# A kernel with its column product by seven products, and its operations placed by engine time

## The chip, the cores and the metric

The kernel runs on one core of a Trainium2 chip. The metric is the device time of one execution in microseconds: 985.84 us, the median of three runs (985.45 to 986.24). The page and the trace are those of one profiled execution.

## The reference, cut to what matters

```python
S, D, F = 2048, 640, 1536            # float32 throughout
xn = layernorm(x)                    # x: [S, D]
a  = xn @ dft_hid_re.T               # the product over the columns (real, imaginary)
b  = xn @ dft_hid_im.T
s  = dft_seq_re @ a - dft_seq_im @ b # the product over the rows
g  = silu((silu(xn @ w_gate) * (xn @ w_up)) @ w_down)
out = x + s * g
```

The kernel exchanges the two transforms: it multiplies by the rows' matrices first and by the columns' after.

## The kernel before, in words

**Number format.** TensorE multiplies float32r operands. Each operand is split into a high part (ACT, `split`, L196: a copy into float32r) and a low part (DVE, L201 or L203: the operand minus its high part). A product of two split operands is three matmuls (`mm3`, L217 to L219): high by high, high by low, low by high.

**Stages, in the order in which PE works.** All products are on transposed tiles of 128 partitions by `TC` = 512 columns; `j` is 0 or 1 and takes chunks `j` and `j + 2` of the 2048 rows.

- `seq(0)` to `seq(3)`: the product over the rows, by the seven-product (Strassen) scheme, for the two halves `j` and for the real and imaginary matrix. Left operands come from `in_cs`; some are added to a tile by accumulating loads that POOL issues (L581). The results go to `p_dram`.
- `hid(j)`: the product over the columns. For each of two chunks it takes ten blocks of `p_dram` (five real, five imaginary) by the five column blocks of the DFT matrix (`in_hd`), ten by five products, and adds them up in five PSUM banks. The right sides are loaded and split again for each `j`. The results go to `y_dram`.
- `gate_up(j)`: the two products with `w_gate` and `w_up` by the seven-product scheme, in twelve rounds `f`. Its left side, the layer-normed input, is made by `xn_t(j)`; `gate_weights` adds and splits each round's weights. In the rounds of `j` = 0 the generator `spare` also makes the operands of `w_down` and stores them (`d_p...` and `d_d...`).
- `down(j)`: the product with `w_down` by the function `strassen` (products p1, p2, p5, p6, p3, p7, p4; next to p1, p2, p5 and p4 runs a "direct" product for the fifth column block, with d1, d2, d1 and d3), whose weights SP fetches back (`fetch`, L1017). Each result passes a silu on ACT, is multiplied by the tile from `y_dram` and added to x on DVE, and is stored.

The order is hid(0), gate_up(0), down(0), hid(1), gate_up(1), down(1).

**What sets the order.** Nothing runs when it is recorded. `Plan` collects every operation with a time: `step` is a piece of PE's work at the running clock `now` (0.226 us for each matmul), `prod` an operation `lead` microseconds ahead of `now`, `post` one behind it. The leads are written by hand (`split(9, ...)`, `LEAD`, `OPEN_T`). `add` moves an operation back only as far as its data demands. The operations, sorted by these times, are issued in that order to the in-order queues of the engines; SP and POOL issue the transfers. Nothing waits for its planned time: an instruction runs as soon as its queue reaches it and its data and buffer are there. `place` and `fit` give each buffer an address in an arena ("hl" for split operands, "raw" for the rest) by the planned lifetimes; a buffer that takes the bytes of an older one waits until that one's last reader is done. Normalised x (`xn`, 40 KB of each partition) lies in "raw".

**The end of hid and the start of gate_up.** gate_up's first two products go to banks 7 and 6, and its third to bank 7 again, so the first product must have been evicted by ACT (L245) by then.

Of the kernel before, what the change touches and what calls it, by code (L numbers as in the profile page):

```python
# [22 lines left out]
MM = 0.226  # L23
HL_KB, RAW_KB, TURN_KB = 83, 95, 28


class Plan:

    def __init__(self):
        self.ops, self.size, self.wrote, self.read = [], {}, {}, {}
        self.now = 0.0
# [8 lines left out]
    def add(self, when, fn, reads=(), writes=(), hold=0.0):  # L45

        reads, writes = list(reads), list(writes)
        t = when
        for k in reads:
            t = max(t, self.wrote.get(k, t))  # L50
        for k in writes:
            t = max(t, self.wrote.get(k, t), self.read.get(k, t))
        for k in reads:
            self.read[k] = max(t, self.read.get(k, t))
        for k in writes:
            self.wrote[k] = t
        names = {k[:2] if k[1] in ("h", "l") else k[0] for k in reads + writes}
        self.ops.append((t, len(self.ops), fn, names, t + hold))
        return t

    def prod(self, lead, fn, reads=(), writes=(), hold=0.0):
        self.add(self.now - lead, fn, reads, writes, hold)

    def step(self, n, fn, reads=(), writes=()):
        t = self.add(self.now, fn, reads, writes, n * MM)
        assert t <= self.now + 1e-6, (t, self.now, [k for k in reads if self.wrote.get(k, 0) > self.now])
        self.now += n * MM

    def post(self, fn, reads=(), writes=(), after=0.0, hold=0.0):
        self.add(self.now + after, fn, reads, writes, hold)  # L70

    def place(self, limits):
# [8 lines left out]
        where = {}  # L81
        for arena, limit in limits.items():
            mine = [(n, self.size[n][1], *v) for n, v in life.items() if self.size[n][0] == arena]
# [9 lines left out]
            found = [f for f in (self.fit(sorted(mine, key=o), limit, p) for p, o in tries) if f]  # L93
# [3 lines left out]
            order, last = best[3], best  # L97
            for _ in range(24):
                hurt = sorted((n for n in last[2] if last[2][n] > 9), key=lambda n: -last[2][n])
                moved = {n: i for i, n in enumerate(hurt[:6])}  # L100
                order = sorted(order, key=lambda m: moved.get(m[0], 99))
                last = next((f for f in (self.fit(order, limit, pauses[a:]) for a in range(len(pauses))) if f), None)
                if last is None:
                    break
                best = min(best, last, key=lambda f: f[0])
            where |= best[1]
        return where

    @staticmethod
    def fit(mine, limit, pauses):  # L110

        placed, where, cost = [], {}, {}
        for n, size, ta, ia, tb, ib in mine:
            near = sorted((o, e, xa, ja, xb, jb) for o, e, xa, ja, xb, jb in placed
                          if (ja <= ib and ia <= jb) or (xa < tb + 8 and ta < xb + 8))
            for pause in pauses:
# [22 lines left out]
def tile_fnet_swiglu(  # L139
# [16 lines left out]
    nc = tc.nc  # L156
# [18 lines left out]
    def raw(name, a=0, n=None):  # L175
        o = where[name]
        arena, size = pl.size[name]
        return space[arena][:, o + a:o + (size if n is None else a + n)]

    def hl(name, i, a=0, n=None):  # L180

        key = name, "hl"[i]
        o = where[key]
        arena, size = pl.size[key]
        return space[arena][:, o + a:o + (size if n is None else a + n)]

# [68 lines left out]
    def strassen(tag, groups, get, top, dop, result, end=False):  # L255
# [16 lines left out]
        def operand(p, g, src):  # L272
# [3 lines left out]
            split(9, s, n, lambda: raw(name, a, n), [key])  # L276
# [13 lines left out]
        def accumulate(dst, src, n):  # L290
            (dn, da, dk), (sn, sa, sk) = dst, src
            pl.prod(12, lambda: nc.vector.tensor_tensor(raw(dn, da, n), raw(dn, da, n), raw(sn, sa, n), op=ALU.add),
# [40 lines left out]
        def s_1(g):  # L333
            X[g], V[g] = get(21, g), get(22, g)
# [7 lines left out]
        def s_2(g):  # L342
            accumulate(W[g], Y[g], n[g])
            return operand("p6", g, W[g])
# [5 lines left out]
        def s_3(g):  # L350
            accumulate(Y[g], X[g], n[g])
# [19 lines left out]
        def a22(g):  # L371
# [769 lines left out]
```

## Time and profile before

| | |
|---|---|
| median of three runs | 985.84 us |
| the profiled execution's own time | 985.85 us |
| its span (first to last instruction) | 984.1 us |
| mean granted TensorE clock | 1.000 |
| matmul instructions (PE) | 4300 |
| DMA | 184.54 MB, mean 188 GB/s |
| transfers that SP issues (queue q1) | 131.35 MB |
| transfers that POOL issues (queue q0) | 52.45 MB |

How to read the answers that are quoted below: a group's row has the line of the kernel, engine, operation, what it writes and reads, its shape, how often it runs, its busy time in us and the mean ns of one, then the idle time of that engine just before these instructions and what ended it. A row of the stretches has start and end in us, then the busy time of PE, PEld, DVE, ACT and POOL (with counts), the granted clock, the DMA share and GB/s. A row of the timeline has start, duration, engine, line, operation, shapes and, in brackets, the idle time before it and its releaser. "SPq" is the queue in which SP issues transfers; "to landing" runs from issue to the last byte.

### The profile page before, as it was taken

The page shows a single profiled execution, that of the slowest core. Times are in us where ns is not written, and L with a number is a line of the kernel's source. Part 1 is how long each engine was busy: PE and PEld are TensorE (multiplying, and loading weights), DVE is VectorE, ACT ScalarE, POOL GpSimd, SP SyncE. Part 2 cuts the span into 40 slices and gives each one's busy share as a digit, 9 for nine tenths or more (in the row PEclk, how much of TensorE's full clock was granted, in tenths as well). Part 3 has the DMA queues.
Part 4 walks back from the last instruction along what each step waited for, and adds up shares of the span by engine and source line. Part 5 has one row for each costly group of instructions (what it writes and reads, how often), then busy time and mean ns, then how long its engine had stood idle before and what let it go on. Part 6 is the DMA issues. An engine that isn't in the chain of part 4 may idle for free.

```text
span 984.1 us, 11734 instructions
## 1 busy us (share of the span) xinstructions
PE 976.2 (99%) x4300; PEld 803.5 (82%) x4300; DVE 700.2 (71%) x936; ACT 483.8 (49%) x706; POOL 106.5 (11%) x173
## 2 busy tenths in 40 slices
PE   9999999999999999999999999999999999999998
PEld 5888888888888888888788888888888888888886
DVE  6889769656865686377678887596578566665675
ACT  5786446444555464334655555343335544444342
POOL 0460220011001100010111211000010000000000
PEclk9999999999999999999999999999999999999999
DMA  9986788474848487540636547679950311125674
GB/s 340 289 209 178 232 243 253 147 210 121 228 141 222 121 238 241 205 172 25 219 134 231 203 144 250 215 242 353 302 204 27 107 55 54 53 75 176 194 264 185
DMA packets 73977, 184.54 MB, mean 188 GB/s; under 512 B 6720, under 2 KB 23360, under 8 KB 73920
## 3 DMA queue, kind: packets, MB, share of 16 engines
q1 hardware_dynamic: 59808, 131.35, 40.1%
q0 software_dynamic: 14112, 52.45, 18.6%
q8 instruction: 33, 0.54, 0.2%
q14 instruction: 24, 0.20, 0.1%
HBM read 149.42 MB, written 34.36 MB: 187 GB/s over the span
## 4 chain that ended last, share of the span: by engine, by line
PE 99%; DVE 0%; ACT 0%; issue 0%; DVEq 0%
PE ps L217 33%; PE ps L219 33%; PE ps L218 33%; PE ps L460 1%; PE ps L228 1%; DVE hl L201 0%; ACT L1088 0%; ACT raw L245 0%; DVE hl L203 0%; DVE raw L1059 0%; DVE raw L1061 0%; ACT hl L196 0%; ACT raw L1055 0%; DVE raw L914 0%; ACT z L1088 0%
## 5 line engine op out<-in xcount | busy, mean ns | idle before, releaser
L196 ACT ACTIVATE hl<-raw 128x1024 fp32r<-128x1024 f32 (+7 forms) x499 | 361.1, 766 | 299.4 <-PE ps L219 79.1
L201 DVE TENSOR_TENSOR hl<-raw,hl 128x1024 fp32r<-128x1024 f32 (+5 forms) x428 | 377.0, 908 | 142.6 <-ACT hl L196 75.8
L217 PE MATMUL ps<-hl 128*128 128x512 f32 x1088 | 422.4, 388 | 0.0
L219 PE MATMUL ps<-hl 128*128 128x512 f32 x1088 | 422.0, 388 | 0.0
L218 PE MATMUL ps<-hl 128*128 128x512 f32 x1088 | 422.0, 388 | 0.0
L218 PEld LDWEIGHTS ps<-hl 128*128 128x128 f32 x1088 | 204.3, 188 | 42.3 <-issue 0.2
L217 PEld LDWEIGHTS ps<-hl 128*128 128x128 f32 x1088 | 204.2, 188 | 42.1 <-issue 0.2
L219 PEld LDWEIGHTS ps<-hl 128*128 128x128 f32 x1088 | 204.2, 188 | 42.0
L217 PE MATMUL ps<-hl,hl 128*128 128x512 f32 x336 | 131.1, 390 | 1.0 <-ACT raw L245 1.0
L219 PE MATMUL ps<-hl,hl 128*128 128x512 f32 x336 | 130.7, 389 | 0.0
L218 PE MATMUL ps<-hl,hl 128*128 128x512 f32 x336 | 130.7, 389 | 0.0
L245 ACT ACTIVATE raw<-ps 128x512 f32<-128x512 f32 (+1 forms) x120 | 78.3, 671 | 97.4 <-PE ps L219 92.5
L250 DVE TENSOR_TENSOR raw<-ps,raw 128x512 f32<-128x512 f32 (+1 forms) x93 | 74.7, 804 | 52.0 <-PE ps L219 50.6
L217 PEld LDWEIGHTS ps<-hl,hl 128*128 128x128 f32 x336 | 63.1, 188 | 14.9 <-ACT raw L245 1.5
L219 PEld LDWEIGHTS ps<-hl,hl 128*128 128x128 f32 x336 | 63.1, 188 | 13.2
L218 PEld LDWEIGHTS ps<-hl,hl 128*128 128x128 f32 x336 | 63.1, 188 | 13.1
L203 DVE SCALAR_TENSOR_TENSOR hl<-raw,hl 128x384 fp32r<-128x384 f32 (+4 forms) x71 | 41.3, 581 | 14.0 <-issue 5.7
L1001 DVE TENSOR_TENSOR raw<-raw 128x512 f32<-128x512 f32 x24 | 16.6, 692 | 47.8 <-ACT raw L1000 47.8
L914 DVE TENSOR_TENSOR raw<-raw 128x256 f32<-128x256 f32 (+1 forms) x96 | 47.9, 520 | 0.0
L581 POOL DMA_DIRECT2D raw<-in_cs x36 | 32.1, 964 | 124.7 <-DVE raw L584 65.6
L658 POOL DMA_DIRECT2D p_dram<-raw x24 | 17.4, 765 | 204.3 <-DVE raw L250 164.9
L1063 POOL DMA_DIRECT2D out<-raw x10 | 6.7, 673 | 293.9 <-ACT hl L196 172.4
(55 smaller groups left out, 307.5 us busy)
## 6 DMA issues: line engine op xcount, KB each, us to landing
raw<-in_cs SPq DMA_DIRECT2D x82, 512.0 KB, 7.0
hl<-d_p SPq DMA_DIRECT2D x56, 384.0 KB, 4.0
raw<-in_cs POOLq DMA_DIRECT2D x36, 512.0 KB, 9.7
raw<-in_wb SPq DMA_DIRECT2D x24, 640.0 KB, 4.1
d_p<-hl POOLq DMA_DIRECT2D x28, 384.0 KB, 3.0
raw<-p_dram SPq DMA_DIRECT2D x8, 1280.0 KB, 9.5
p_dram<-raw POOLq DMA_DIRECT2D x16, 512.0 KB, 6.6
raw<-in_hd SPq DMA_DIRECT2D x20, 320.0 KB, 7.8
```

The lines of the kernel that those rows point to most:

```text
L196: nc.scalar.activation(like(hl(dst, 0, a, n)), src(), AF.Copy, scale=1.0 if scale is None else scale)
L201: nc.vector.tensor_tensor(lo, src(), hi, op=ALU.subtract)
L203: nc.vector.scalar_tensor_tensor(lo, src(), scale, hi, op0=ALU.mult, op1=ALU.subtract)
L217: nc.tensor.matmul(o, w(0), m(0), start=first, stop=False, skip_group_check=True)
L218: nc.tensor.matmul(o, w(0), m(1), start=False, stop=False, skip_group_check=True)
L219: nc.tensor.matmul(o, w(1), m(0), start=False, stop=True, skip_group_check=True)
L245: pl.post(lambda: nc.scalar.activation(wide(raw(dst, a, n)), pair(b), AF.Copy), pkeys(b), [(dst, a)], after)
L250: pl.post(lambda: nc.vector.tensor_tensor(wide(raw(dst, a, n)), pair(b), wide(raw(other)), op=op), [*pkeys(b), (other, 0)], [(dst, a)], after)
L581: pl.prod(lead, lambda: nc.gpsimd.dma_start(wide(raw(name)), source(q, g), accum_op=ALU.add), [], [(name, 0), (name, 1)], 8)
L658: pl.post(lambda: nc.gpsimd.dma_start(p_dram[ri, c, e0:e0 + len(b)].rearrange("k p t -> p k t"), wide(raw(name))), [(name, 0)], [("pd", ri ...
L914: pl.prod(lead, lambda o=o, a=a, b=b, op=op: nc.vector.tensor_tensor(o(), a(), b(), op=op), [(w, 0)], [(c, lead)])
L1001: pl.post(lambda: nc.vector.tensor_tensor(raw(o, at, TC), raw(g2), raw(u), op=ALU.mult), [(g2, 0), (u, 0)], [(o, at)])
```

## The change: what it does

1. **`hid_s(j)` replaces `hid(j)`.** The column product of the two chunks `j` and `j + 2` becomes one call of `strassen`, with the ten blocks in groups of 3 and 2, the real and imaginary blocks as the two halves of the inner dimension, and columns 0 to 255 and 256 to 511 as the two halves of the outer one; the last 128 columns are the direct products. The sums of the right sides are made and split once, kept in `T`, and used for both `j`. Sums of left blocks come from accumulating loads on POOL (`fold`) or from DVE.
2. **Order of the stages:** hid_s(0), hid_s(1), gate_up(0), down(0), gate_up(1), down(1).
3. **`Plan.schedule`** gives times to all operations but those of `seq(0)`, which keep their leads. It records each operation once with `Probe`, which catches the shape and works out a duration (a rate and a base for each engine, 390 KB per us for a transfer, 215 for an accumulating one), builds the dependencies, places results forward from PE's times, and then places every `prod`, from the last to the first, as late as its readers allow and where its engine's lane (`Lane`) is free: 2.5 us before PE needs it, 0.25 before another engine does. A transfer gets 2.0 us for landing and 2.5 to spare, and is put 0.8 us earlier in the order.
4. **Arenas:** `xn` lies in two tiles of 20 KB beside the arenas; once its last reader is done their room goes to split operands, and later a part of it to "raw" (`raw3`).
5. **`down(0)`** adds x by an accumulating load on POOL in place of a load and a DVE addition. Row statistics are loaded in one transfer for each half, and `xn_t` takes one sum from another pair of terms.

All instructions of the changed kernel have the one line of the recording helper, L82.

```diff
-MM = 0.226
-HL_KB, RAW_KB, TURN_KB = 83, 95, 28
+MM = 0.22667
+RATE, RATE_ADD = 390, 215
+SPARE, SPARE_PE, SPARE_DMA, STRETCH = 0.25, 2.5, 2.5, 1.04
+HL_KB, RAW_KB, TURN_KB = 86,80,20
...
+    def last(self, due, n):
+        t = due - n
+        for i in range(bisect(self.at, due) - 1, -1, -1):
+            if self.at[i] < t + n and self.end[i] > t:
+                t = self.at[i] - n
+            if i and self.at[i] < t - 60:
+                break
+        return t
...
+        delay = lambda i: 2.0 if engine[i] == "dma" else 0.2
...
+        for i in reversed(range(n)):
+            if ops[i][0] not in ("prod", "store"):
+                continue
+            lane, long = lanes[engine[i]], took[i] * STRETCH
+            spare = SPARE_DMA if engine[i] == "dma" else SPARE
+            due = min([start[j] - (SPARE_PE if engine[j] == "pe" and spare < SPARE_PE else spare) for j in after[i]],
+                      default=ops[i][1] + 20)
+            if ops[i][5]:
+                due = min(due, ops[i][5])
+            t = lane.last(due - delay(i), long)
+            if t < soon[i]:
+                t = lane.first(soon[i], long)
+                t = t if t < soon[i] + 6 else soon[i]
+            start[i] = t
+            lane.put(t, long)
...
+    def hid_s(j):
...
+        def grow(what, other):
+            pl.prod(22, lambda: nc.vector.tensor_tensor(raw(R[what]), raw(R[what]), raw(R[other]), op=ALU.add),
+                    [(R[other], 0)], [(R[what], 0)])
...
+        def block(q, g):
+            return p_dram[q % 10 - 1, j + 2 * (q // 10 - 1), 3 * g:3 * g + 3 - g].rearrange("k p t -> p k t")
...
+        def fold(q, dst, g, lead):
+            name = dst[0]
+            pl.prod(lead, lambda: nc.gpsimd.dma_start(wide(raw(name)), block(q, g), accum_op=ALU.add),
+                    [("pd", q % 10 - 1, j + 2 * (q // 10 - 1))], [(name, 0)], 8)
...
+        strassen(("hid", j), [3, 2], get, top, dop, result, pairs=pairs[1 + j:] + pairs[:1 + j], fold=fold, ahead=12)
...
+            fold = j == 0
+            fold or pl.post(lambda: nc.sync.dma_start(
                 part(raw(res)), xt[c, e0:e0 + len(b), :, at:at + w].rearrange("k p t -> p k t")), [], [(res, 0)], -8)
...
+            if fold:
+                pl.post(lambda: nc.gpsimd.dma_start(
+                    part(raw(name)), xt[c, e0:e0 + len(b), :, at:at + w].rearrange("k p t -> p k t"), accum_op=ALU.add),
+                    [], [(name, 0)], late + 1)
...
     for k in range(4):
+        pl.fixed = k == 0
         seq(k)
         if k == 0:
             store_rows()
     for j in range(2):
-        hid(j)
+        hid_s(j)
+    pl.back = pl.now
+    for j in range(2):
         gate_up(j)
         down(j)
```

**ACT, at the end of the column product and the start of gate_up(0).** `hl` and `hl2` are split operands, `ps` is PSUM; the 128x256 and 128x384 rows are splits of gate_up's first weights. Before:

```order
L196 ACTIVATE hl_74<-raw_75 128x512
L196 ACTIVATE hl_74<-raw_75 128x1024
L196 ACTIVATE hl2_2549<-raw_75 128x256
L196 ACTIVATE hl2_2549<-raw_75 128x384 x2
L196 ACTIVATE hl2_2549<-raw_75 128x256
L196 ACTIVATE hl_74<-raw_75 128x256
L245 ACTIVATE raw_75<-ps_76 128x512
L196 ACTIVATE hl_74<-raw_75 128x256
L245 ACTIVATE raw_75<-ps_76 128x512 x6
```

The same place now:

```order
L82 ACTIVATE hl_74<-raw_75 128x256
L82 ACTIVATE hl_74<-raw_75 128x384
L82 ACTIVATE hl_74<-raw_75 128x1024 x2
L82 ACTIVATE hl_74<-raw_75 128x384
L82 ACTIVATE hl_74<-raw_75 128x256
L82 ACTIVATE raw_75<-ps_76 128x1024
L82 ACTIVATE raw_75<-ps_76 128x512 x3
```

Before, one split of the second round's weights stands ahead of gate_up's first eviction (the first 128x512 row from `ps`), and six further evictions, hid's and gate_up's, follow; now two splits of the first round's weights and one 128x1024 eviction, the last result of hid_s(1), stand ahead of the first eviction.

**SP, in down(0), ahead of the product p4 and the direct product d3.** `d_p4_0` and `d_p4_1` are the two halves of p4's stored weights, `d_d3_0` and `d_d3_1` those of d3, each fetched in a high and a low piece; `y_dram`, `in_xt` and `in_wb` are other inputs; the brackets name the engines or transfers that a load waits for. Before:

```order
L1051 DMA raw_75<-y_dram_99 128x2x512 [waits DMAHW7_49]
L1017 DMA hl_74<-d_p4_0_88 128x768 [waits DMAHW0_49,PE_49]
L1017 DMA hl_74<-d_p4_0_88 128x768 [waits DMAHW1_49,PE_49]
L1017 DMA hl_74<-d_d3_0_83 128x384 [waits DMAHW2_49]
L1017 DMA hl_74<-d_d3_0_83 128x384 [waits DMAHW3_49]
L1017 DMA hl_74<-d_p4_1_98 128x768 [waits DMAHW4_49]
L1017 DMA hl_74<-d_p4_1_98 128x768 [waits DMAHW5_49,PE_49]
L1017 DMA hl_74<-d_d3_1_93 128x384 [waits DMAHW6_49]
L1017 DMA hl_74<-d_d3_1_93 128x384 [waits DMAHW7_49,PE_49]
```

The same place now:

```order
L82 DMA raw3_3373<-y_dram_99 128x2x512 [waits DMAHW7_49,DVE_49]
L82 DMA hl_74<-d_p4_0_88 128x768 [waits DMAHW0_49,PE_49]
L82 DMA hl_74<-d_p4_0_88 128x768 [waits DMAHW1_49,PE_49]
L82 DMA hl_74<-d_p4_1_98 128x768 [waits DMAHW2_49,PE_49]
L82 DMA hl_74<-d_p4_1_98 128x768 [waits DMAHW3_49,PE_49]
L82 DMA hl_74<-d_d3_0_83 128x384 [waits DMAHW4_49]
L82 DMA hl_74<-d_d3_0_83 128x384 [waits DMAHW5_49]
L82 DMA hl_74<-d_d3_1_93 128x384 [waits DMAHW6_49]
L82 DMA hl_74<-d_d3_1_93 128x384 [waits DMAHW7_49]
```

All four pieces of p4 now stand ahead of the four of d3, each of p4's waiting for PE to leave its buffer; PE still runs d3 first and p4 after it.

362 lines of the change are left out of this document (266 added, 96 removed).

## The prediction

> **What bounds the kernel now.** I read the page first, for the shares and the chain that ended last.
>
> ```profile
> span 984.1 us, 11734 instructions
> PE 976.2 (99%) x4300; PEld 803.5 (82%) x4300; DVE 700.2 (71%) x936; ACT 483.8 (49%) x706; POOL 106.5 (11%) x173
> PE 99%; DVE 0%; ACT 0%; issue 0%; DVEq 0%
> ```
>
> PE is busy for 99% of the span, and the chain is PE's for 99%: no other engine sets the end. Hence two questions: how many matmuls are there, and where does PE wait? The groups by shape answer the first, the chain in order of time gives the pace.
>
> ```profile
> L217 PE MATMUL ps<-hl 128*128 128x512 f32 x1076 | 419.0, 389 | 0.0
> L217 PE MATMUL ps<-hl,hl 128*128 128x512 f32 x336 | 131.1, 390 | 1.0 <-ACT raw L245 1.0
> ```
> ```profile
> 461.94 0.23 PE ps L219
> ...
> 468.74 0.24 PE ps L219
> ```
>
> Each of the three lines of a split product (L217 to L219) has 1076 + 336 full-width matmuls, 4236 in all. One lasts 389 ns, but they overlap: from the first to the last of these two chain rows thirty start, in 6.80 us, so one costs 0.2267 us. That pace, not 389 ns, is the price of a matmul here. The x336 row also holds the only wait of weight on PE, 1.0 us behind an ACT eviction. The timeline there:
>
> ```profile
> 469.08 1.56 DVE L201 TENSOR_TENSOR hl<-raw,hl 128x1024 fp32r<-128x1024 f32 x2 [4.87 <-PE ps L219]
> ...
> 471.02 1.16 DVE L914 TENSOR_TENSOR raw<-raw 128x256 f32<-128x256 f32 x2
> ...
> 471.30 0.39 PE L219 MATMUL ps<-hl 128*128 128x512 f32 x1
> ...
> 471.48 0.72 ACT L196 ACTIVATE hl<-raw 128x256 fp32r<-128x256 f32 x2 [3.67 <-DVE raw L914]
> ...
> 472.11 0.58 ACT L245 ACTIVATE raw<-ps 128x512 f32<-128x512 f32 x1
> ...
> 472.74 0.50 PE L217 MATMUL ps<-hl,hl 128*128 128x512 f32 x1 [1.05 <-ACT raw L245]
> ```
>
> DVE stood 4.87 us for a buffer that PE still read; so L914's weight sum came late, ACT's split behind it too, and the eviction that frees bank 7 stood behind that split in ACT's queue. PE's next start was due at 471.30 + 0.227 = 471.53 and came at 472.74: 1.21 us lost. Twelve matmuls of gate_up precede it, so hid(0) ended at 471.53 - 12 x 0.2267 = 468.81.
>
> **The change part by part.** The profiled execution took 985.85 us, 1.75 more than its span; the median of the runs shown is 985.84, so the sum stands against either.
>
> *The column product.* Before, hid runs 10 blocks x 5 banks x 3 matmuls for each of four chunks: 600. After, each of two calls runs 7 products of 5 blocks x 2 banks x 3 and 4 direct ones of 5 x 3: 210 + 60 = 270, together 540. Sixty fewer at 0.2267 us: **-13.60 us**, all on the path, since PE waits for nothing else there. The Trainium skill (TensorE: Matmul & The Clock Gate, "Wait — 56ns, not 53.3ns?") gives 215.7 ns from start to start for 512 columns; the trace's 226.7 ns does not agree and decides. By the page's figure the term would be -12.94 and the forecast 0.66 us higher.
>
> What it adds lies on DVE, ACT and the queues. DVE's rows:
>
> ```profile
> L201 DVE TENSOR_TENSOR hl<-raw,hl 128x1024 fp32r<-128x1024 f32 x170 | 203.4, 1222 | 78.7 <-ACT hl L196 40.2 <-PE ps L219 16.3 <-issue 12.0
> ...
> L201 DVE TENSOR_TENSOR hl<-raw,hl 128x1536 fp32r<-128x1536 f32 x28 | 49.1, 1756 | 27.7 <-ACT hl L196 15.3 <-PE ps L218 5.6 <-PE ps L219 3.7
> L201 DVE TENSOR_TENSOR hl<-raw,hl 128x512 fp32r<-128x512 f32 x70 | 48.0, 688 | 21.1 <-PE ps L218 7.7 <-ACT hl L196 5.1 <-issue 4.4
> ...
> L250 DVE TENSOR_TENSOR raw<-ps,raw 128x1024 f32<-128x1024 f32 x20 | 24.5, 1223 | 28.6 <-PE ps L219 28.6
> L292 DVE TENSOR_TENSOR raw<-raw 128x1536 f32<-128x1536 f32 x12 | 21.0, 1754 | 0.1
> ...
> L867 DVE TENSOR_TENSOR raw<-raw 128x1024 f32<-128x1024 f32 x16 | 18.9, 1221 | 4.3 <-DMA raw<-in_xt 4.3
> ...
> L201 DVE TENSOR_TENSOR hl<-raw,hl 128x640 fp32r<-128x640 f32 x10 | 8.2, 822 | 9.0 <-ACT hl L196 9.0
> ```
> ```profile
> 400.90:469.90 69.00, 69.00 (x306) 57.15 (x305) 42.21 (x51) 26.60 (x42) 3.46 (x6) 1.00 0.40 140
> 469.90:616.80 146.90, 145.85 (x642) 119.98 (x642) 117.00 (x219) 84.02 (x166) 24.35 (x45) 1.00 0.56 200
> 616.80:690.20 73.40, 73.40 (x326) 60.77 (x325) 53.37 (x42) 28.74 (x27) 3.29 (x5) 1.00 0.79 272
> ```
>
> Before, the two hid take 40 low halves of 512 and 20 of 640 on DVE: 40 x 0.688 + 20 x 0.822 = 44.0 us in 600 x 0.2267 = 136.0. After, 14 low halves each of 1536 and 1024 (14 x 2.978 = 41.7), the right sides once (7 of 1280, estimated between the rows of 1024 and 1536 at 1.49, and 3 of 640: 12.9), sums of the left blocks (4 x 2.976 = 11.9), sums of the right ones (4 x 1.49 + 0.82 = 6.8) and six combined evictions (7.3): 80.6 us in 540 x 0.2267 = 122.4, or 66%. With the next input's preparation (12 x 1.22 plus smaller ones) some 80%. It fits, so I cost it at **0** on the path; if the cover goes, PE waits as at 471.53.
>
> *Both column products first.* gate_up(1) now follows down(0) with no hid between, so its input and first weights are made inside gate_up(0) and down(0): 8 x 1.22 for layer norm, 4 x 1.22 for sums, 7 x 1.22 for low halves, some 27 us with smaller ones, less about 6 us of additions that down(0) gives to POOL's accumulating loads. (117.0 + 53.4 + 21) / 220.3 = 87% at most. Also **0**, with the least reserve of any stretch. An accumulating load there holds only the output store behind it on POOL's queue; no matmul waits for that.
>
> *The entry into gate_up(0).* The old buffer wait goes: **-1.21**. Next late is the same eviction of bank 7: ACT's order now has two weight splits and a 128x1024 eviction ahead of it.
>
> ```profile
> L245 ACT ACTIVATE raw<-ps 128x512 f32<-128x512 f32 x100 | 57.9, 601 | 71.8 <-PE ps L219 67.0 <-DVE hl L201 3.5 <-DMA y_dram<-raw 0.9
> ...
> L245 ACT ACTIVATE raw<-ps 128x1024 f32<-128x1024 f32 x20 | 20.4, 1021 | 25.6 <-PE ps L219 25.6
> ```
>
> PE wants the bank 12 matmuls, 2.72 us, after hid ends. The planner puts the large eviction 2 us after that end: 2.0 + 1.02 + 0.60 = 3.62, so 0.90 late. If ACT runs ahead, bank 7 is free at 1.36 + 0.2 + 0.6 and nothing is lost; if the sums come late as before, 1.2. I take the middle of 0 and 1.2: **+0.6**.
>
> *SP's order in down(0).* Before, the weights of the direct product d3 are fetched between the two halves of p4's, early:
>
> ```profile
> 662.62 0.90 SPq L1017 DMA_DIRECT2D hl<-d_d  x2
> ...
> 664.86 2.00 SPq L1017 DMA_DIRECT2D hl<-d_d  x2
> ```
> ```profile
> 682.93 0.60 ACT L1055 ACTIVATE raw<-ps 128x512 f32<-128x512 f32 x1 [1.82 <-PE ps L219]
> ```
> ```profile
> L1017 SPq DMA_DIRECT2D hl<-d_d x24: 319/422/636, 598.7 to 955.1; - x24
> ...
> DMA to landing us min/median/max: 2.3/4.0/7.0
> ```
> ```profile
> hl<-d_d SPq DMA_DIRECT2D x24, 192.0 KB, 4.3
> ```
>
> At 682.93 ACT evicts what d3's 18 matmuls (4.08 us) made, so they began near 678.4: over 13 us in hand. After, all four d3 loads stand behind p4's last piece, which waits on PE. By the planner's addresses that piece takes the bytes of p7's first weights, free when half of p7 is done, 18 matmuls or 4.08 us before d3 starts. SP issues one load per 0.45 us, so d3's first pair goes out 3.6 and 3.2 us ahead of need, the second needed two matmuls later still. At the median landing of 4.3 PE waits 0.7 to 1.1, at the shortest 2.3 nothing, at the longest 7.0 some 3.4. I take the median: **+1.0**.
>
> *Placing by free time.* The rest of the order moves by a few places, and the first product over rows keeps its hand-set leads. The planner's transfers are the risk (third rival); between nothing and that, I take **0**. The end of down(1) keeps its operations.
>
> Sum: 985.85 - 13.60 - 1.21 + 0.6 + 1.0 = **972.6 us**.
>
> **The rivals.**
> *No new wait (0.20).* ACT runs ahead and d3 lands in 3 us: 985.85 - 13.60 - 1.21 = 971.0. For it: shortest landing 2.3; against: the median 4.3. The Trainium skill (DMA: Bandwidth & Descriptors, "Anatomy of one DMA", fitted on the gpsimd path) puts a transfer at 2.0 us plus bytes / 436e3, an estimate of 2.45 us for d3's 192 KB; by that page d3 costs nothing. SP's median row speaks against it.
>
> *Several short waits (0.20).* In the two stretches at 80 to 87% DVE some buffer comes free late, as at 469.08. One such wait cost 1.21 us; the 21 products of both hid_s and down(0) have one occasion each; at 2 to 9 of them, 972.6 + 2.4 to 10.9 = 975 to 983.5. For it: fuller DVE. Against: before, DVE idled 78.7 + 27.7 + 21.1 us ahead of its low halves (the rows above), and PE lost 1.21 by it.
>
> *Accumulating loads too late, slower (0.05).*
>
> ```profile
> L581 POOL DMA_DIRECT2D raw<-in_cs x36: 851/888/1870, 24.0 to 346.8; - x36
> ...
> DMA to landing us min/median/max: 5.3/9.7/15.8
> ```
>
> The planner lets such a load go 2.54 + 2.0 + 2.5 + 0.8 = 7.8 us before its split, with about 2.7 us to spare until PE. Place: p5 and p7 of the row products, and the eight new ones of hid_s. Beyond a landing of 10.5 us PE waits, at most 5.3 each. If 10 of some 40 land halfway, 2.65 late, that is 26.5 us: 971.0 + 26.5 = 997.5. It decides from a total of 14.8 us on. Against: a queue issues as soon as its buffer is free, not at the planned time, and before, with the same landings, PE never waited.
>
> *The change does less than it says:* excluded, since the built program has 4176 full-width matmuls for 4236.
>
> **How the numbers follow.** Forecast 0.55 (971.3 to 975), then 0.20, 0.20, 0.05. The range 970.9 to 978.0 holds the forecast, the first rival and a third of the second. About 0.2%, 2 us, is what a measurement tells from no change: faster 0.94 (all but the third rival and a hundredth of the second), same 0.02 (that hundredth and one of the third), slower 0.04.
>
> The Trainium skill (TensorE: Matmul & The Clock Gate, Part 1) says that about 3.4 us without matmuls halves the array's clock; no wait of this trace is that long, and only d3's longest landing would be.
>
> **What would show it.** Right: 4240 matmuls, a span near 971, PE's waits two, at gate_up(0)'s third product and before d3 in down(0) near 678.4 - 6.8 (thirty matmuls fewer) + 61.2 (270 more ahead) = 733 us; DVE's share about 75%. Wrong: PE waiting inside hid_s for DVE or DMA, waits in the row products behind accumulating loads, or a pace other than 0.2267.

## The result and the profile after

The changed kernel takes 971.63 us (median of four runs, 970.70 to 972.00), the kernel before took 985.77 beside it (985.45 to 986.24). The ratio is 0.9855, with a 95% interval of 0.9838 to 0.9872: about 14 us, or 1.4%, faster. The profiled execution took 971.28 us.

The page's first lines and its chain:

```profile
span 969.5 us, 11543 instructions
PE 962.3 (99%) x4240; PEld 792.9 (82%) x4240; DVE 733.9 (76%) x927; ACT 489.3 (50%) x676; POOL 119.5 (12%) x179
PE 99%; ACT 0%; DVE 0%; issue 0%
```

Sixty matmuls fewer, as counted beforehand, and VectorE at 76%. What PE waited for, and PE's part of the chain in order of time:

```profile
PE ps L82 <- ACT z L82: 2.3, 1, 2.3
```
```profile
2.28 962.35 PE ps L82 x4240
```

Apart from the start, PE waits nowhere: all 4240 matmuls are one piece of 962.35 us. It ends at 964.63, and the last ACT instruction begins at 964.65; before, that instruction begins at 979.60. The difference is 14.95 us; sixty matmuls and the old wait make 13.60 + 1.21 = 14.81. That is the first rival, "no new wait", to 0.2 us.

So close a match is in part luck. The warm-up, sixteen matmuls at the start, does not take equally long in every execution: the 17th matmul starts at 8.39 us here and at 8.01 before, and between 7.4 and 8.6 in the traces of all runs. Counted from the 17th matmul the change is worth 15.3 us, 0.5 more than the sum. Of this, 0.4 are five small gaps in the trace before, 0.03 to 0.11 us each, near 473, 532 and 593 us.

The two places at which a new wait was expected. ACT at the entry into gate_up(0), near 523 us:

```profile
517.46 5.52 ACT L82 ACTIVATE hl<-raw 128x256 fp32r<-128x256 f32 x10
523.76 1.03 ACT L82 ACTIVATE raw<-ps 128x1024 f32<-128x1024 f32 x1 [0.79 <-PE ps L82]
525.12 0.60 ACT L82 ACTIVATE raw<-ps 128x512 f32<-128x512 f32 x1 [0.33 <-PE ps L82]
```

The brackets tell it: ahead of both evictions ACT stood idle, for PE. The splits that stand ahead in its queue were done by 523.0, so PE did not wait for ACT, ACT waited for PE. It was close: bank 7 was free at 525.12 + 0.60 = 525.72, and PE's thirteenth matmul of gate_up(0), the first that writes bank 7 again, starts at 526.29, some 0.5 us later.

SyncE in down(0), and the landing of d3's four loads:

```profile
719.60 8.25 SPq L82 DMA_DIRECT2D hl<-d_p  x4
727.90 1.85 SPq L82 DMA_DIRECT2D hl<-d_d  x4
```
```profile
DMA to landing us min/median/max: 3.2/3.7/4.3
```

Here the mechanism is the one that was worked out: p4's loads block SyncE, d3's go out at 727.90. They landed in 3.2 to 4.3 us (the first two, which PE needs first, in 3.2 each), and PE did not stop. How close that was, the fourth experiment shows.

### The profile page after: what moved, and what is told of

It is laid out like the page before. It is cut to its first block, busy times and chain, and to the rows that moved or that the text cites. A ratio compares the mean times of both kernels' runs of the same rounds, so it can differ in the third digit from the quotient of the medians.

```text
span 969.5 us, 11543 instructions
## 1 busy us (share of the span) xinstructions
PE 962.3 (99%) x4240; PEld 792.9 (82%) x4240; DVE 733.9 (76%) x927; ACT 489.3 (50%) x676; POOL 119.5 (12%) x179
## 4 chain that ended last, share of the span: by engine, by line
PE 99%; ACT 0%; DVE 0%; issue 0%
PE ps L82 99%; ACT L82 0%; DVE raw L82 0%; ACT raw L82 0%; ACT z L82 0%
## 5 line engine op out<-in xcount | busy, mean ns | idle before, releaser
L82 PE MATMUL ps<-hl 128*128 128x512 f32 (+1 forms) x3277 | 787.9, 388 | 0.0
L82 PEld LDWEIGHTS ps<-hl 128*128 128x128 f32 x3277 | 613.9, 188 | 127.0 <-issue 0.2
L82 DVE TENSOR_TENSOR hl<-raw,hl 128x1024 fp32r<-128x1024 f32 (+5 forms) x360 | 346.6, 994 | 137.2 <-ACT hl L82 92.9
L82 ACT ACTIVATE hl<-raw 128x1024 fp32r<-128x1024 f32 (+6 forms) x416 | 325.8, 826 | 169.2 <-DVE raw L82 91.7
L82 PE MATMUL ps<-hl,hl 128*128 128x512 f32 (+1 forms) x935 | 257.5, 388 | 0.0
L82 ACT ACTIVATE raw<-ps 128x512 f32<-128x512 f32 (+1 forms) x144 | 97.7, 681 | 235.3 <-PE ps L82 230.6
L82 DVE TENSOR_TENSOR raw<-raw 128x256 f32<-128x256 f32 (+7 forms) x236 | 193.0, 843 | 18.3 <-ACT raw L82 15.2
L82 PEld LDWEIGHTS ps<-hl,hl 128*128 128x128 f32 x935 | 175.3, 188 | 36.1
L82 DVE TENSOR_TENSOR raw<-ps,raw 128x512 f32<-128x512 f32 (+1 forms) x95 | 77.2, 814 | 50.9 <-PE ps L82 50.1
L82 ACT ACTIVATE hl<-xn 128x1024 fp32r<-128x1024 f32 (+3 forms) x61 | 42.4, 723 | 13.0 <-PE ps L82 10.2
L82 POOL DMA_DIRECT2D p_dram<-raw x24 | 16.4, 685 | 248.5 <-DVE raw L82 210.3
L82 ACT ACTIVATE raw<-raw 128x512 f32<-128x512 f32 (+1 forms) x30 | 21.5, 718 | 45.9 <-DVE raw L82 44.6
L82 DVE TENSOR_TENSOR hl<-xn,hl 128x1024 fp32r<-128x1024 f32 (+3 forms) x50 | 40.8, 833 | 3.6 <-PE ps L82 3.5
L82 POOL DMA_DIRECT2D raw<-in_cs x36 | 32.2, 987 | 77.6 <-DMA raw<-in_cs 45.6
L82 DVE SCALAR_TENSOR_TENSOR hl<-raw,hl 128x256 fp32r<-128x256 f32 (+4 forms) x56 | 32.8, 586 | 4.2 <-ACT hl L82 4.2
L82 POOL DMA_DIRECT2D out<-raw x10 | 6.9, 685 | 225.0 <-DVE raw L82 189.4
L82 DVE TENSOR_TENSOR raw<-raw,raw 128x512 f32<-128x512 f32 (+3 forms) x30 | 29.0, 973 | 4.7 <-ACT raw L82 4.1
L82 POOL DMA_DIRECT2D d_p<-hl x28 | 15.2, 543 | 71.3 <-ACT hl L82 60.1
L82 DVE BATCH_NORM_STATS2 bst<-xn 128x6 f32<-128x320 f32 x32 | 13.7, 480 | 5.0 <-DMA xn<-in_x 5.0
L82 POOL DMA_DIRECT2D y_dram<-raw x12 | 8.2, 682 | 64.8 <-DVE raw L82 46.4
L82 POOL DMA_DIRECT2D raw<-in_xt x6 | 6.9, 1210 | 72.1 <-DVE raw L82 72.1
L82 ACT ACTIVATE xn<-xn,sm,rowst 128x640 f32<-128x640 f32 x16 | 14.2, 912 | 3.0 <-DVE sm L82 2.0
```

The lines of the kernel that those rows point to most:

```text
L82: return real(*args, **kw)
```

## The experiments

Theory: the gain is the sixty matmuls at PE's pace plus the one old wait, and all that the product adds on VectorE, ACT and the queues lies under PE. First rival: placing by free time is itself a part of the gain. Second rival: the product's side work is not covered in general, but by luck of the order.

### Undoing the product (first and fifth)

```diff
     for j in range(2):
-        hid_s(j)
+        hid(j)
```

> The changed kernel with the old column product put back (both halves first, placing by free time and all else kept; 4300 matmuls again). Theory (the gain is sixty matmuls at the pace of TensorE plus the 1.21 us wait, and nothing else): 971.3 + 60 x 0.2267 = 984.9 us, TensorE without a wait. Rival (placing by free time itself gave part of the gain, by shorter waits that the sum doesn't know): under 984 us. Second rival (the old product, which loads and splits its right sides twice, doesn't fit the planner's order): waits on TensorE, over 986.5 us.

Measured: 1015.91 us (1014.17 to 1016.75), ratio 1.0299, interval 1.0284 to 1.0315. The second rival of that text seemed right, but the cause could be another. The room that the old product's buffers found in the arena was bad: their addresses came from a few random orders, and by the plan 373 reuses of split operands' room came before the old buffer's end (26 in the changed kernel). So the same program once more, with addresses from a longer search, a table in place of `fit`:

```diff
+            if arena in AT:
+                mine.sort(key=lambda m: (m[3], m[5], str(m[0])))
+                where |= {m[0]: 8 * o for m, o in zip(mine, AT[arena], strict=True)}
+                continue
```

> The first experiment again (the changed kernel with the old column product), but its buffers have addresses from a longer search: in the first experiment 373 of the reuses in the arena of split operands were planned before the old buffer's planned end (26 in the changed kernel), here hardly any. Theory (the gain is sixty matmuls and one wait; the first experiment lost its 30 us to buffers taken too early): 984.9 us, within 1.5, TensorE with hardly a wait. Rival (the old product, with its right sides loaded and split twice, does not fit this order, whatever the addresses): over 1000 us again.

Measured: 984.18 us (983.65 to 984.72), ratio 0.9982, interval 0.9973 to 0.9991. The page's line of the engines and PE's waits with the first addresses:

```profile
PE 985.2 (97%) x4300; PEld 804.0 (79%) x4300; DVE 696.5 (69%) x930; ACT 482.8 (48%) x706; POOL 111.7 (11%) x179
```
```profile
PE ps L82 <- ACT raw L82: 8.7, 4, 4.1
PE ps L82 <- DVE hl L82: 6.2, 12, 0.7
PE ps L82 <- DVE raw L82: 4.9, 4, 1.4
```

and with the searched ones:

```profile
PE 976.2 (99%) x4300; PEld 804.0 (82%) x4300; DVE 697.1 (71%) x930; ACT 479.4 (49%) x706; POOL 112.1 (11%) x179
```
```profile
PE ps L136 <- ACT z L136: 2.3, 1, 2.3
```

The engines run the same number of instructions in both; 31.7 us came from addresses alone. How, the waits of ACT and DVE ahead of their splits tell, with the first addresses and with the searched ones:

```profile
ACT hl L82 <- PE ps L82: 261.3, 106, 23.7
DVE hl L82 <- PE ps L82: 120.0, 51, 8.5
```
```profile
ACT hl L136 <- PE ps L136: 90.0, 35, 8.7
DVE hl L136 <- PE ps L136: 11.4, 8, 2.9
```

A split needs nothing from PE but the room that it writes into. With the first addresses the splits idled 381 us for such room, with the searched ones 101, and only in the first case did some of it reach PE. The old product under the new plan costs 984.18, and 984.9 was the theory's number. Against the two kernels below with the new product and searched addresses (971.09 and 970.86), the product is worth 13.1 to 13.3 us; 60 x 0.2267 = 13.6.

### The product alone (second, seventh and ninth)

Into the kernel before goes `hid_s` with hand-set leads; the order of the stages and the arenas' kind stay, so the right sides are made for each half.

```diff
-HL_KB, RAW_KB, TURN_KB = 83, 95, 28
+HL_KB, RAW_KB, TURN_KB = 79, 99, 28
...
+    def hid_s(j):
+        R = {}
+        T.clear()
...
-        hid(j)
+        hid_s(j)
```

> The kernel before with the seven-product column product alone: hand-set leads, old order of the stages (the second column product after down(0)), right sides made anew for each half, old arenas. 4234 matmuls (six of the warm-up are fewer). Theory (only the sixty matmuls matter, VectorE has room for the sums and low halves even with the right sides made twice): 985.8 - 13.6 = 972.2 us, at most 1.2 less if the old wait at the entry into gate_up(0) goes too, at most 2 more if one or two buffers come free late. Rival (without placing by free time the operands come late in a full stretch): several waits on TensorE, 975 to 984 us.

Measured: 1028.08 us (1027.19 to 1029.12), ratio 1.0426. The rival, and worse than it.

> The second experiment again (the kernel before with the seven-product column product alone, right sides made for each half, hand-set leads), with the products of the second half in the same order as those of the first, so that the sums of its right sides are the right ones (in the second experiment the second half of the output was built from wrong sums; the amount of work was the same). Theory (VectorE, which makes right sides twice and the next input in the same stretch, is over its time; the order of the products does not matter): 1022 to 1034 us, the waits again in the two stretches of the column product. Rival (the waits came from the other order in the second half): under 1010 us.

Measured: 1027.64 us (1026.61 to 1027.76), ratio 1.0421. So the order of the products is not it. In both runs the products of the first half read the buffers that hold the right sides of the second, so these two kernels do not give the output of the kernel before; the amount of work is the same. The ninth run binds each product to its own buffers (shown against the seventh; the direct products in the same way) and takes its addresses from the longer search:

```diff
-            return (lambda g, kk, e, i: hl(T[p], i, e * D + (3 * g + kk) * P, P)), (lambda g: both(T[p]))
+            t = T[p]
+            return (lambda g, kk, e, i: hl(t, i, e * D + (3 * g + kk) * P, P)), (lambda g: both(t))
```

> The kernel before with the seven-product column product alone (hand-set leads, old order of the stages, right sides made for each half), once more: each product now reads the right sides of its own half (in the two runs before, the first half read the buffers meant for the second), and the buffers' addresses come from the longer search. Theory (VectorE: 93% busy in the column product of the first half there, since it makes the right sides twice and prepares gate_up's input in the same stretch): 1000 us or more, TensorE waiting for VectorE's low halves in both stretches of the column product. Rival (those waits came from buffers and their addresses, and sixty matmuls fewer is all that matters): 972 to 978 us.

Measured: 1028.49 us (1026.92 to 1029.21), ratio 1.0428, interval 1.0413 to 1.0444. So neither the buffers' names nor their addresses were it. Nor do the splits idle longer for room than in the kernel before: 122.8 us on ACT and 50.0 on DVE, against 138.6 and 51.4. PE's page line and its waits:

```profile
PE 979.8 (95%) x4240; PEld 799.7 (78%) x4240; DVE 755.0 (74%) x948; ACT 502.2 (49%) x686; POOL 113.4 (11%) x173
```
```profile
PE ps L281 <- DVE hl L264: 22.3, 10, 6.7
PE ps L280 <- DVE raw L987: 11.7, 2, 6.4
PE ps L280 <- DVE raw L313: 3.3, 2, 2.0
PE ps L280 <- ACT hl L259: 2.7, 2, 1.6
```

The loss adds up. The waits make 22.3 + 11.7 + 3.3 + 2.7 = 40.0 us, and PE is busy for 979.8 - 962.3 = 17.5 us longer with the same 4240 matmuls (the granted clock, below): 57.5. The spans of the two profiled executions differ by 1026.5 - 969.5 = 57.0.

What DVE did ahead of one such wait (L264 low halves; L1021 the layer norm of gate_up(0)'s input; L355 sums of left blocks), and PE's row:

```profile
428.26 1.22 DVE L1021 TENSOR_TENSOR raw<-raw 128x1024 f32<-128x1024 f32 x1
...
431.06 2.35 DVE L1021 TENSOR_TENSOR raw<-raw 128x1024 f32<-128x1024 f32 x2
...
436.13 1.29 DVE L1021 TENSOR_TENSOR raw<-raw 128x512 f32<-128x512 f32 x2
...
439.88 0.69 DVE L1021 TENSOR_TENSOR raw<-raw 128x512 f32<-128x512 f32 x1
440.48 1.75 DVE L264 TENSOR_TENSOR hl<-raw,hl 128x1536 fp32r<-128x1536 f32 x1
```
```profile
442.29 0.59 PE L281 MATMUL ps<-hl,hl 128*128 128x512 f32 x1 [2.98 <-DVE hl L264]
```

DVE has no gap here, and 1.22 + 2.35 + 1.29 + 0.69 = 5.55 us of it go to an input that gate_up(0) needs some 30 us later. The low half that PE needs at 439.3 stands behind them, and PE waits 2.98. In all, this layer norm takes 12.2 us in that stretch (the groups from 409.8 to 475 us):

```profile
L1021 DVE TENSOR_TENSOR raw<-raw 128x1024 f32<-128x1024 f32 x8 | 9.5, 1220 | 0.0
...
L1021 DVE TENSOR_TENSOR raw<-raw 128x512 f32<-128x512 f32 x4 | 2.7, 687 | 0.0
```

And hid(0) as a whole, from its first matmul to its last; the columns are start, end and length, then PE, PEld, DVE, ACT and POOL busy:

```profile
400.37:481.00 80.63, 66.77 (x271) 53.05 (x270) 67.54 (x61) 34.63 (x37) 6.50 (x8) 0.92 0.50 155
```

DVE has 67.54 us of work there, and the 270 matmuls would take 270 x 0.2267 = 61.2: the theory's "over its time" is so for this half. Without the 12.2 us that are not due yet it would be 55.3; the eleventh run hides 53.84. In the second half, where 22.8 of the 40.0 us of waits lie, the chain goes back past DVE to a load of a right side:

```profile
714.01 22.55 DMA raw<-in_hd
```

It took 22.55 us to land, where these loads take 3.9 to 7.9 in the changed kernel, and DVE's nearly gapless work for this half begins only behind it. So for the second half the cause is a late load as well as VectorE's share, and the two are not parted.

### VectorE made fuller, with the placing (eleventh and twelfth)

```diff
-                nc.vector.tensor_tensor(lo, src(), hi, op=ALU.subtract)
+                for _ in range(2 if not nc.dry and dst[0] == "S" and isinstance(dst[1], tuple) and dst[1] == ("hid", 0) and dst[3] == 0 else 1):
+                    nc.vector.tensor_tensor(lo, src(), hi, op=ALU.subtract)
```

(in the twelfth with `("down", 0)` and without the `isinstance`; the plan does not know of the repeats)

> The changed kernel with seven of the low halves of the first column product (the blocks of three, 128x1536) computed twice on VectorE, the second result the same as the first: 7 x 1.756 = 12.3 us more, which brings VectorE from 42.8 to 55.1 us in the 61.2 us of that stretch (70 to 90%). Theory (the added VectorE work of the column product lies wholly under TensorE's): 971.6 us, no wait on TensorE. Rival (VectorE's order there has hardly any time to spare, so that each repeat comes late by up to 1.76 us): 974 to 984 us, with waits between 410 and 540 us.

> The same in down(0): seven low halves of 128x1536 computed twice, 12.3 us more on VectorE between 640 and 752 us, where it is busy for 97.4 of 112.5 us (87%, then 97%). Theory (cover of 15 us, of which 12.3 are used, and lumps of 1.76 against some 2.5 us of planned reserve): at most two waits of 1 to 2 us, 971.6 to 975 us. Rival (the reserve in the fullest stretch is used up): three or more waits, 976 us or more, with TensorE waiting for VectorE between 650 and 760 us.

Measured: 971.30 us (970.81 to 971.98), ratio 0.9851, and 972.87 us (972.41 to 973.41), ratio 0.9867. The first column product of the eleventh run, then down(0) of the twelfth:

```profile
400.80:462.00 61.20, 61.20 (x272) 50.67 (x271) 53.84 (x39) 28.96 (x26) 7.94 (x9) 1.00 0.69 203
```
```profile
670.10:743.50 73.40, 72.77 (x322) 59.90 (x321) 71.06 (x58) 31.53 (x30) 5.62 (x7) 1.00 0.79 256
```

With 53.84 us of DVE's work in 61.20 (88%) PE does not stop once. In down(0) VectorE reaches 97%, and PE's waits in that run are these two:

```profile
668.74 0.73 PE L82 MATMUL ps<-hl 128*128 128x512 f32 x2 [0.84 <-DVE raw L82]
...
733.35 6.89 PE L82 MATMUL ps<-hl 128*128 128x512 f32 x29 [0.63 <-DMA hl<-d_d]
```

One wait of 0.84 us is VectorE's; the other is d3's, whose loads need nothing of VectorE. The eleventh run has a wait for d3's loads too, 0.77 us at 732.52, so its "no wait on TensorE" is not met to the letter; in the column product, which it was about, there is none. The first theory of both texts held. What was not tried is the second half, where VectorE has 53.87 us without any addition (below).

### The placing taken away (sixth, third and tenth)

In the sixth run the lanes are left out: an operation is put where its readers need it, whether its engine is free then or not. Transfers have a lane as well, so they lose it too.

```diff
-            t = lane.last(due - delay(i), long)
-            if t < soon[i]:
-                t = lane.first(soon[i], long)
-                t = t if t < soon[i] + 6 else soon[i]
+            t = max(due - delay(i) - long, soon[i])
```

> The changed kernel, but every operation that prepares something is placed by the time at which its readers need it alone, not where its engine is free (two operations may have the same time on one engine); addresses again from the longer search, arenas 84 and 82 KB. Product, order of the stages and matmuls unchanged. Theory (the order of the queues is what counts, and an order by need is nearly the same): 971.3 to 973 us. Rival (in the stretches where VectorE is busy for 85 to 90% its work piles up ahead of the need): several waits on TensorE for VectorE, 976 us or more, most of them between 410 and 750 us.

Measured: 993.07 us (991.57 to 995.00), ratio 1.0074, interval 1.0060 to 1.0088. The rival, at 22 us more than the searched addresses give with lanes. Its longest wait of PE, and DVE ahead of it:

```profile
475.73 1.23 DVE L134 TENSOR_TENSOR hl<-raw,hl 128x1024 fp32r<-128x1024 f32 x1 [9.55 <-ACT hl L134]
476.87 11.57 DVE L134 TENSOR_TENSOR raw<-raw 128x1024 f32<-128x1024 f32 x12
488.36 1.75 DVE L134 TENSOR_TENSOR hl<-raw,hl 128x1536 fp32r<-128x1536 f32 x1
...
490.17 5.55 PE L134 MATMUL ps<-hl 128*128 128x512 f32 x17 [7.65 <-DVE hl L134]
```

and the same block in the changed kernel:

```profile
464.80 12.32 DVE L82 TENSOR_TENSOR raw<-raw 128x1024 f32<-128x1024 f32 x12
```

Twelve additions for gate_up's input (a layer norm and its sums) run in one block in both. By need alone DVE first idles 9.55 us for an operand, then the block starts at 476.87, and a low half that PE waits for stands behind it; with lanes the block starts 12 us earlier, and PE does not wait for what follows it. But the delay does not begin with VectorE. The chain shows what the operand waited for:

```profile
454.23 20.39 DMA raw<-p_dram
```

A load of two left blocks (512 KB) took 20.39 us to land; it went out behind two loads of 1280 KB each, at 452.7 and 453.2. The median of such 512 KB loads is 5.9 us in the changed kernel. The next long wait of PE, 3.84 us at 706.24, goes back in the same way to a load that took 11.98 us. So the rival's time came true, but not its reason alone: loads crowded together and VectorE's block behind them made the two longest waits, and the run takes both lanes away at once. Room is not the reason: the splits idle for it 58.0 us on ACT and 1.8 on DVE, less than in the tenth run (67.5 and 15.7).

In the third and tenth run only the row products lose the placing:

```diff
-        pl.fixed = k == 0
+        pl.fixed = True
         seq(k)
...
+        pl.fixed = False
```

> The changed kernel with all four row products at their hand-set leads, where the planner sets three of them; the rest is placed by free time as before. Theory (the row products had no wait before and have none now, so placing them by free time is worth nothing): 971.3 us, within 1 us, TensorE waiting for nothing in the first 410 us. Rival (the planner's places relieve a transfer or VectorE there): 973 us or more, with waits in the row products.

Measured: 1024.47 us (1018.51 to 1024.79), ratio 1.0374. Neither text fits: but for 2.9 us, PE's waits (35 us in all, without the start) lie after 410 us, where no lead was touched. With searched addresses in arenas of the same size:

> The third experiment again (all four row products at their hand-set leads, all else placed by free time), with addresses from the longer search. Theory (the row products need no placing; the third experiment lost its time to buffers taken too early): 971 to 972 us, TensorE without a wait up to 410 us. Rival (hand-set leads do cost something in the row products): 974 us or more, with waits there.

Measured: 971.09 us (970.45 to 971.51), ratio 0.9848, interval 0.9832 to 0.9865; PE waits only at the start. In the row products placing is worth nothing, and the third run lost its time to addresses, as the first did (its splits idle for room 220.5 us on ACT and 62.0 on DVE, against 67.5 and 15.7 in the tenth).

### d3's loads, later and earlier (fourth and eighth)

```diff
+                def go(i=i):
+                    for x in range(8 * (p == "d3" and j == g == i == 0 and not nc.dry)):
+                        nc.sync.dma_start(z.bitcast(F32)[:, x * 16:x * 16 + 16], xt[0, 0, :, x * 16:x * 16 + 16])
+                    nc.sync.dma_start(hl(name, i).bitcast(F32), d_dram[p, g][:, i * n:i * n + n])
...
+                pl.prod(14 - 4 * g, go, [("dd", p, g, i)], [(name, "hl"[i], 0)])
```

> The changed kernel with eight small loads (128x16 each, into a scratch tile that nobody reads) put on SyncE's queue just ahead of the first load of the direct product d3's weights in down(0): eight issues of some 0.45 us each, so d3's loads go out 3.6 us later. Theory (d3's loads went out 3.7 and 3.3 us ahead of need and landed in 3.2 to 4.3, so there was hardly any reserve and the term of 1.0 us was a near miss): TensorE waits once, near 732 us, for 3 to 4 us, 974.3 to 975.3 us in all. Rival (need comes later than worked out, with 2 us or more in reserve): a wait under 1.6 us, under 973 us.

Measured: 978.11 us (977.84 to 978.98), ratio 0.9920, interval 0.9905 to 0.9935. SyncE and PE:

```profile
727.33 3.77 SPq L82 DMA_DIRECT2D z<-in_xt  x8
731.14 2.16 SPq L82 DMA_DIRECT2D hl<-d_d  x4
```
```profile
736.19 14.16 PE L82 MATMUL ps<-hl 128*128 128x512 f32 x53 [5.00 <-DMA hl<-d_d]
```

The loads went out at 731.14, 3.24 us later than in the changed kernel, and landed in 4.5 to 5.0 us, the first of them in 5.0. PE stopped at 736.19 - 5.00 = 731.19. This time can't be set against 727.90 as it stands, for PE runs earlier in this execution by its shorter warm-up (17th matmul at 7.71 us, in the changed kernel's trace at 8.39). The same matmul, d3's first, starts at 731.65 in the changed kernel's trace, 3.7 us after its first load went out there, as the text above worked it out; its first two loads had landed at 731.10 and 731.58, and the second is needed two matmuls later, at 732.10. So the reserve in the changed kernel was some 0.5 us. The wait is longer than expected, since the first landing took 5.0 us in place of 3.2; and the run lost 6.5 us, not 5.0, by the clock (below).

The other direction: d3's loads due 10 us earlier, with searched addresses.

```diff
+                pl.bound = pl.now - 10 if h == 3 else None
                 for g in range(2):
                     fetch(p, g)
+                pl.bound = None
```

> The changed kernel with the loads of d3's weights due 10 us earlier, which puts them ahead of p4's on SyncE's queue in both down stages, and addresses from the longer search. Theory (d3's loads landed just in time, so in some executions TensorE waits a little): 970.5 to 971.3 us, at most 1 us faster than the changed kernel, and no execution above 971.5. Rival (nothing waits for d3 in any execution): 971.6 us within the spread of the changed kernel's own times.

Measured: 970.86 us (970.56 to 971.17, five runs), ratio 0.9847, interval 0.9834 to 0.9861. SyncE there:

```profile
711.71 4.73 SPq L134 DMA_DIRECT2D hl<-d_d  x4
...
719.25 4.88 SPq L134 DMA_DIRECT2D hl<-d_p  x4
```

d3's loads go out 13 to 16 us earlier. The median is 0.8 us below the changed kernel's, and the five runs lie within 0.6 us where the changed kernel's four lie within 1.3; the two intervals of the ratio overlap. It is the fastest kernel of this study. How much of the 0.8 us is d3's and how much the addresses', these runs do not part: in the tenth run, too, other addresses let d3's loads go out at 723.74, four microseconds earlier than in the changed kernel. A third candidate is the warm-up, which differs by up to a microsecond between traces: in the two profiled executions, neither of which waits for d3, PE takes 955.95 us from the 17th matmul's start to the last one's in the changed kernel and 955.97 here. So these traces show no gain in PE's work; that d3's loads cost the changed kernel anything in the executions without a trace is likely by the eleventh and twelfth run, but not shown.

## Why the prediction was right, point by point

**Sixty matmuls at 0.2267 us, -13.60: right.** PE's end moved by 14.95 us for 14.81 of the two large terms (15.3 without the warm-up); undoing the product alone gives 13.1 to 13.3.

**The old wait, -1.21: right.** It is gone from the trace, and the old product under the new plan, which has no wait either, is 1.9 us faster than the kernel before (0.9 to 2.7 by the interval).

**The entry into gate_up(0), +0.6: did not come.** The step said that the 128x1024 eviction is planned 2 us after the column product's end. A planned time holds nothing back, as the text itself had said of transfers: ACT ran it when PE was done, and waited 0.79 us for that. "ACT runs ahead", the lower end, was the case, with some 0.5 us in hand.

**d3's loads, +1.0: right in kind, too large.** Issue, order and need were as worked out (3.7 us from the first load to the need, for 3.6), only the landing of the two loads needed first was 3.2 us and not the 4.3 of the median over all such loads. That is just in time: 0 in the profiled execution, 0.77 and 0.63 in the profiles of the eleventh and twelfth run, in which the same SyncE order stands. The term's end at 2.3 us of landing was nearer than the median. For the sum, the profiled execution is the first rival (971.0 for 971.28 measured), and the median of all runs lies 0.6 above that rival and 1.0 below the forecast. That 971.63 falls inside the forecast's 971.3 to 975 is in part luck: the two waits that set the forecast apart from the first rival, 1.6 us together, are both absent from the trace. The two large terms were right by their mechanism.

**VectorE in the column product, 66%, with the next input some 80%: right.** The two halves in the changed kernel:

```profile
400.80:462.00 61.20, 61.20 (x272) 50.69 (x271) 42.07 (x32) 28.36 (x26) 7.95 (x9) 1.00 0.76 207
462.00:523.20 61.20, 61.20 (x272) 50.69 (x271) 53.87 (x51) 28.17 (x32) 7.82 (x9) 1.00 0.59 179
523.20:670.10 146.90, 146.90 (x650) 121.68 (x649) 125.05 (x223) 83.37 (x162) 22.35 (x41) 1.00 0.50 178
670.10:743.50 73.40, 73.40 (x326) 60.79 (x325) 61.81 (x51) 33.18 (x33) 6.76 (x7) 1.00 0.83 265
```

(42.07 + 53.87) / 122.4 = 78%, and (125.05 + 61.81) / 220.3 = 85% in gate_up(0) and down(0), for "87% at most".

**"It fits, so I cost it at 0": the right number from too weak a reason.** The step took a share below 100% over both halves for cover. What covers the work is in which stretch it stands, and behind what: the plan puts the next input's preparation into the half in which no right sides are made (42.07 and 53.87 us above). In the product alone it stands in the half in which right sides are made, 67.54 us for 61.2, and in the sixth run the same work, 12 us later and behind a late load, ends in a wait of 7.65. The second rival, several short waits, is what happens then: 16 waits of 2.5 us on average in the product alone, twice the 1.21 that it reckoned with, and the clock besides.

**Placing by free time, 0: right for this comparison, but not idle.** It hardly makes the kernel faster by itself: with the old product, the new order, plan and addresses together bring 1.9 us, little more than the old wait. It is what lets the new product's work be hidden; without the lanes, VectorE's and the transfers' together, the kernel takes 993.07. How much of the loss of the product alone belongs to the hand-set leads, how much to the right sides being made twice and how much to the old order of the stages was not parted: no run makes them twice under the planner.

**Accumulating loads too late: did not come.** PE waits for none, in the changed kernel or in the tenth run.

## What to carry to other kernels

Where PE's chain is the whole time, count PE's instructions and price them at their pace; the sum is then as good as the list of waits. A helper engine's busy share does not tell whether added work is hidden: look stretch by stretch at what stands in its queue ahead of the operation that PE needs next, at whether its loads go out in a crowd, and at the plan's addresses, because room for which the splits had to wait cost 32 and 53 us here, with the same number of instructions on every engine. A load that lands just in time is a term of its spread, not of its median: move its issue a few places ahead and the question is gone.

## What the runs showed of the hardware

A longer wait costs more than itself. After the 5.00 us wait of the fourth run the stretches show the granted clock (the number behind POOL's count):

```profile
736.10:739.50 3.40, 3.31 (x8) 2.64 (x9) 1.40 (x2) 0.06 (x1) 1.20 (x1) 0.50 1.01 335
739.50:743.00 3.50, 3.50 (x16) 2.82 (x15) 0.00 (x0) 0.55 (x1) 0.00 (x0) 0.90 1.06 389
```

At 0.50 eight matmuls start in 3.4 us, one every 0.43 us in place of 0.2267; PE ends at 736.19 + 234.97 = 971.16 in place of 964.63, 6.5 us later, after a warm-up that was 0.7 us shorter: so the stop cost 7.2 us, 5.2 of them by the late start of d3's first matmul and 2.0 by the slow matmuls behind it. In the product alone this share is 17.5 us beside 40.0 of waits. The Trainium skill (TensorE: Matmul & The Clock Gate, Part 1) says that the array falls to half its clock after an idle window of about 3.4 us and stays there until it has been busy for about as long, with windows that run freely; its 426.7 ns from start to start in that state agrees with the 0.43 us here. Its length of idle time does not decide here. All waits of 3.8 us and more in these runs were followed at once by half the clock. Of the shorter ones some were: 2.98 us in the ninth run (the row at 442.29 above, half the clock until 445.6), 2.76 in the first, 1.98 in the third. Others were not: 2.98 us in the seventh run, 2.38 in the sixth. The same wait for the same matmul, 2.33 us in the second run and in the seventh, shows both; the three microseconds behind it in each:

```profile
434.60:437.60 3.00, 3.00 (x7) 2.42 (x8) 3.00 (x3) 0.00 (x0) 0.00 (x0) 0.50 1.04 214
```
```profile
434.20:437.20 3.00, 2.99 (x13) 2.49 (x14) 3.00 (x3) 0.00 (x0) 0.00 (x0) 1.00 1.07 214
```

Seven matmuls start in the one, thirteen in the other. A window that runs freely could make such a difference, by where the wait falls in it; no run here tests that.

The other surprise is how much addresses weigh. The same instructions with other addresses took 1015.91 and 984.18 us, and 1024.47 and 971.09 us.
